# Loading v in one piece a partition, and a new order of steps, in a linear-attention and gated-FFN kernel

## The chip, the cores and the metric

The kernel runs on one core of a Trainium2 chip. A core has five engines with queues of their own: TensorE (PE, matmuls; its weight loads are shown as PEld), VectorE (DVE), ScalarE (ACT), GpSimd (POOL) and SyncE (SP), which here issues all DMAs. The core's 16 DMA engines move data between HBM and the on-chip memory. Each engine works through its instructions in the order in which the program lists them, and waits where an operand isn't ready. The metric is the device time of one execution in microseconds (us), a median of runs; the profile is of one execution.

## What is computed

```python
# q, k, v: (8, 8, 576, 64) float32 (batch, heads, positions, head size)
q_s = exp(q - max(q, axis=-1));  q_s = q_s / (sum(q_s, axis=-1) + 1e-9)
k_s = exp(k - max(k, axis=2));   k_s = k_s / (sum(k_s, axis=2) + 1e-9)
kv  = einsum('bhsd,bhse->bhde', k_s, v)
x   = einsum('bhsd,bhde->bhse', q_s, kv)          # then (B, S, H*D): 4608 tokens x 512
...
xn  = x / sqrt(mean(x * x, axis=-1) + 1e-6) * rms_g
g   = xn @ w_gate                                  # 512 x 1536
out = (g * sigmoid(g) * (xn @ w_val)) @ w_out      # 1536 x 512
```

## The kernel before

The 4608 tokens are nine blocks of 512 (j = 0 to 8), the eight heads four pairs (g = 0 to 3), the eight batches b = 0 to 7 of 576 positions each. A block of tokens needs the key-value products of the one or two batches that it touches, so attention work for later batches and blocks runs between the matmuls of the FFN.

The work is cut into 2,950 named steps (`k_exp.5.1`, `pp.3.0.4` and so on), and a table, `ORDER`, lists them. A step's arguments are numbers, a letter behind a colon names the engine (A for ACT, D for DVE, P for POOL). The kernel records the steps in that order, so `ORDER` alone sets the order on each engine's queue.

**Keys and values.** For a batch b >= 1 and head pair g, `k_load`, `v_load` and `kd_load` bring k, v and a transposed k. Position 5p + i sits in partition p, so a tile has 116 partitions of five positions. `kd` has one buffer, `kt` three, `vt` two. `k_max` (DVE, line 514) takes the maximum of `kd`; `k_rows` spreads it on PE; `k_sub` and `k_exp` (line 539) follow; `k_mm` (PE, line 566) multiplies with v. `k_seg.m` is a `k_mm` and a `k_rows` of neighbouring pairs in one accumulator. The tile of v is (116, 5, 2, 65): the 65th word of each row is a one, so that `k_mm` gives the sum of the keys' exponentials as well. `v_ones` (POOL, line 510) writes the ones, `v_load` (line 507) the 64 words beside them:

```python
nc.sync.dma_start(t[:, :, :, :D], v[b - 1, g].rearrange("p (j h d) -> p j h d", h=2, d=D))
...
nc.gpsimd.memset(v_tile(b, g)[:, :, :, D:], 1.0)
```

In `ORDER` of before, `v_ones` stands ahead of `v_load` of the same tile.

**Queries.** For blocks j >= 2, `q_load` (SP, line 638) brings a 128 x 512 tile (three buffers); `q_max` (DVE, line 697), `q_half`, `q_max2`, `q_sub`, `q_exp` (ACT, line 718), `q_sum`, `q_rec`, `q_mul`, `q_t` (DVE, line 741) make the softmax, `q_hi`, `q_lo`, `q_x` (PE, line 762) the attention output in two halves of precision, `x_sq`, `x_acc` and `n_...` the norm.

**FFN.** Blocks 2 to 8 use products `pp.j.u.n` (PE, line 1132: 12 matmuls, u = 0 to 5 a sixth of the hidden size, n = 1 to 7), evictions `ev.j.u.n` (ACT copies and activations, DVE additions, lines 381, 1147 to 1156), the split of the hidden tile `hu_hi` (ACT), `hu_lo` (DVE or POOL, line 1168), and `fu.j.u.n.k` (PE, line 1180: six matmuls into the output). `ps_gv`, the accumulators of `pp`, are two: a late eviction stops PE two products on. Blocks 0 and 1 use `f1`, `f1p`, `f2` (lines 1195, 1209, 1263); the weights come in the first 95 us (`load_w`, line 422) and are converted, normed and split. `store` (line 1283) brings the output out.

Of the kernel before, what the change touches and what calls it, by code (L numbers as in the profile page):

```python
# [29 lines left out]
k_exp.0.2 k_max.0.3 load_w.0.0 q_eps0.0.0 q_exp.0.1 k_eps.0.2 k_max.0.1 k_exp.0.3 k_mm.0.0 load_w.0.1 q_rec0.0.0  # L30
q_sum0.0.3 q_mul0.0.0:P kv_norm0.0.0:A k_rec.0.2 q_sum0.0.1 k_exp.0.1 q_t0.0.0 load_w.1.1 q_eps0.0.3 k_tr0.2.0
k_eps.0.3 q_c0.0.0:A q_rec0.0.3 k_eps.0.1 k_tr0.2.1 k_rec.0.1 q_mul0.0.3:P k_ev0.2.0 k_rec.0.3 q_x0.0.0 q_max0.0.2
k_ev0.2.1 load_w.1.0 q_eps0.0.1 k_mm.0.2 q_rec0.0.1 q_sub0.0.2:P x_sq.0.0 g_abs k_tr0.3.0 kv_norm0.0.2:A q_mul0.0.1:P
k_tr0.3.1 n_sum0.0 q_exp.0.2 load_w.3.2 k_ev0.3.1 q_sum0.0.2 k_tr0.1.0 conv_mul.0.0 q_eps0.0.2 conv_low.0.0.1
q_rec0.0.2 q_mul0.0.2:P k_ev0.3.0 load_w.2.0 conv_shift.0.0 conv_low.0.1.1 k_tr0.1.1 k_mm.0.3 conv_sign.0.0 k_ev0.1.0
s_tr x_hi.0.0:A s_top load_w.0.2 q_t0.0.3 s_rows q_c0.0.3:A x_lo.0.0 kv_norm0.0.3:A q_t0.0.1 s_bits k_ev0.1.1 k_mm.0.1
load_w.2.1 q_c0.0.1:A q_x0.0.3 conv_low.1.0.2 load_w.1.2 conv_mul.0.1 kv_norm0.0.1:A conv_shift.0.1 x_hi.0.3:A
q_x0.0.1 conv_sign.0.1 kd_load.1.0 x_sq.0.3 q_t0.0.2 x_lo.0.3 w_hi.0.0.2:P conv_mul.1.0 load_w.3.0 q_c0.0.2:A
conv_shift.1.0 x_hi.0.1:A q_x0.0.2 conv_sign.1.0 conv_low.0.2.1 x_lo.0.1 w_lo.0.0:P load_w.4.1 f1.0.0.0.0 conv_mul.1.1
f1.0.0.0.1 f1.0.0.0.3 f1.0.1.0.0 x_hi.0.2:A f1.0.1.0.1 conv_shift.1.1 f1.0.1.0.3 w_lo.0.1:P conv_low.2.0.2 f1.0.0.0.2  # L40
conv_sign.1.1 load_w.2.2 f1.0.0.1.0 f1.0.0.1.1 f1.0.1.0.2 x_lo.0.2 f1.0.1.1.0 w_hi.1.0.2:P conv_mul.0.2 f1.0.1.1.1
n_sq.0.0 conv_shift.0.2 f1.0.0.1.2 f1.0.0.1.3 q_load0.1.0 f1.0.1.1.2 f1.0.0.2.0 conv_sign.0.2 f1.0.0.2.1 x_sq.0.1
f1.0.1.1.3 f1.0.1.2.0 load_w.3.1 k_max.1.0 f1.0.1.2.1 conv_mul.2.0 w_lo.1.0:P n_sum0.1 x_sq.0.2 conv_shift.2.0
f1.0.1.2.2 conv_low.1.2.1 f1.0.1.2.3 w_lo.1.1:P conv_sign.2.0 f1.0.0.2.2 kd_load.1.1 f1.0.0.2.3 conv_low.3.2.1
# [1297 lines left out]
```

## Time and profile before

| what | value |
|---|---|
| median of 3 runs (lowest to highest) | 984.56 us (984.31 to 988.42) |
| the profiled execution, its span | 984.37 us, 982.6 us |
| PE, DVE, ACT, POOL busy | 917.1, 623.3, 573.6, 260.1 us |
| mean granted clock of PE, as a share of full speed | 0.977 |
| DMA packets, of these under 512 B | 57,437, 35,552 |
| moved | 66.18 MB |

The span runs from the first to the last instruction; 1.8 us of the execution lie around it. Busy times are summed instruction by instruction. A bracket behind a row of the timeline tells how long the engine had been idle before it and what ended the wait. An engine's idle time costs only where the end of the program depends on it.

### The profile page before, as it was taken

To read this page: it belongs to the slowest core of one execution; us is meant where nothing else is said; L and a number is where in the kernel's file an instruction comes from. 1 tells how busy PE (TensorE), PEld (TensorE's weight loads), DVE (VectorE), ACT (ScalarE), POOL (GpSimd) and SP (SyncE) were. 2 spreads that over 40 slices of the span, in tenths; PEclk is the share of its full clock that TensorE was granted. 3 is DMA by queue.
4 is the path that set the end of the run, shared out by engine and by line. 5 is a ranking of instruction groups with operands and counts; after the bars stand their busy time and mean duration, and the time that the engine had idled before them with its cause. 6 is when DMAs were issued, how large, how long until landed. Compare 5 with 4: busy or idle time off the path is not lost.

```text
span 982.6 us, 16263 instructions
## 1 busy us (share of the span) xinstructions
PE 917.1 (93%) x6426; PEld 646.1 (66%) x6426; DVE 623.3 (63%) x1350; ACT 573.6 (58%) x896; POOL 260.1 (26%) x263
## 2 busy tenths in 40 slices
PE   8798998999799899778998699999999999999998
PEld 6465876444358677555676477777587776777764
DVE  5786877687588688655665588563868635623322
ACT  6876967896567658554565477463675535433331
POOL 4443764726553222005212020000323101100000
PEclk9897999999999999989999899999999999999999
DMA  9787032112323203222003212010211001000101
GB/s 350 233 256 241 14 89 65 56 47 52 103 72 93 81 21 83 55 70 66 11 12 85 90 36 59 24 44 3 68 25 54 1 1 43 1 1 1 44 1 44
DMA packets 57437, 66.18 MB, mean 67 GB/s; under 512 B 35552, under 2 KB 35808, under 8 KB 57360
## 3 DMA queue, kind: packets, MB, share of 16 engines
q1 hardware_dynamic: 57360, 65.14, 22.2%
q8 instruction: 50, 0.82, 0.3%
q14 instruction: 27, 0.22, 0.1%
HBM read 55.69 MB, written 9.44 MB: 66 GB/s over the span
## 4 chain that ended last, share of the span: by engine, by line
PE 70%; DMA 11%; DVE 10%; ACT 4%; POOL 2%; issue 2%; SPq 1%; DVEq 0%; ACTq 0%; POOLq 0%
PE ps_gv L1132 34%; PE ps_o L1180 19%; DMA qt<-in_q_dram 7%; PE ps_gv L1209 4%; PE ps_gv L1195 4%; PE ps_o L1263 4%; DMA w_o<-in_w_dram 2%; PE ps_a L762 2%; PE ps_a L566 1%; DMA kd<-in_kt_dram 1%; DMA vt<-in_v_dram 1%; DVE sw L703 1%; POOL wf L936 1%; PE ps_gv L456 1%; DVE ps_a L446 1%
## 5 line engine op out<-in xcount | busy, mean ns | idle before, releaser
L1132 PEld LDWEIGHTS <-w_gv 128*128 128x128 f16 x2016 | 197.8, 98 | 43.4 <-issue 6.0
L1132 PE MATMUL ps_gv<-xo,w_gv 128*128 128x256 f16 x1296 | 155.6, 275 | 4.1 <-ACT w_br L381 3.3
L1132 PEld LDWEIGHTS <-w_br 128*128 128x128 f16 x756 | 75.7, 101 | 37.1 <-issue 22.9
L1132 PE MATMUL ps_gv<-x_op,w_gv 128*128 128x256 f16 x720 | 86.6, 273 | 0.0
L1180 PEld LDWEIGHTS <-hh 128*128 128x128 f16 x504 | 49.0, 99 | 51.3 <-issue 4.0
L1132 PE MATMUL ps_gv<-xo,w_br 128*128 128x256 f16 x540 | 69.6, 282 | 13.7 <-DVE wf L1147 6.4
L1180 PEld LDWEIGHTS <-hl 128*128 128x128 f16 x504 | 48.9, 98 | 49.1 <-issue 1.6
L1180 PE MATMUL ps_o<-w_o,hh 128*128 128x512 f16 x336 | 79.5, 380 | 0.0
L1180 PE MATMUL ps_o<-w_o,hl 128*128 128x512 f16 x336 | 79.4, 379 | 0.0
L1195 PE MATMUL ps_gv<-xo,wf 128*128 128x512 f32 x288 | 76.7, 422 | 2.2 <-DVE tm L1224 2.0
L1195 PEld LDWEIGHTS ps_gv<-xo,wf 128*128 128x128 f32 x288 | 56.6, 200 | 18.9 <-issue 4.3
L1132 PEld LDWEIGHTS <-wf 128*128 128x128 f16 x504 | 49.3, 98 | 8.3 <-issue 0.2
L381 ACT COPY ps_gv<-ps_gv 128x512 f32<-128x512 f32 x42 | 24.0, 572 | 49.3 <-PE ps_gv L1132 30.7
L697 DVE TENSOR_REDUCE st<-qt 128x16 f32<-128x512 f32 x28 | 19.0, 680 | 46.8 <-DMA qt<-in_q_dram 46.7
L1132 PE MATMUL ps_gv<-xo,wf 128*128 128x256 f16 x360 | 43.7, 273 | 0.0
L510 POOL MEMSET vt<- 116x10 f32 x28 | 3.2, 117 | 135.6 <-PE ps_a L566 101.5
L1147 DVE TENSOR_TENSOR w_br<-ps_gv,w_br 128x512 f32<-128x512 f32 x29 | 19.9, 688 | 28.5 <-PE ps_gv L1132 24.0
L1132 PE MATMUL ps_gv<-x_op,w_br 128*128 128x256 f16 x216 | 27.8, 280 | 7.7 <-DVE w_br L1147 7.5
L718 ACT ACT_TABLE_LOAD x23 | 29.5, 1283 | 7.7 <-DMA qt<-in_q_dram 7.3
L1209 PE MATMUL ps_gv<-x_op,w_br 128*128 128x512 f16 x144 | 32.4, 379 | 0.0
L1147 DVE TENSOR_TENSOR tm<-ps_gv,tm 128x512 f32<-128x512 f32 x29 | 19.9, 686 | 19.5 <-PE ps_gv L1132 16.4
L566 PE MATMUL ps_a<-vt,kt 115*64 115x65 f32 (+1 forms) x560 | 23.3, 231 | 9.1 <-DMA vt<-in_v_dram 9.1
(336 smaller groups left out, 1945.2 us busy)
## 6 DMA issues: line engine op xcount, KB each, us to landing
w_br<-in_w_dram SPq DMA_DIRECT2D x21, 512.0 KB
qt<-in_q_dram SPq DMA_DIRECT2D x35, 256.0 KB
out_dram<-ot SPq DMA_DIRECT2D x34, 256.0 KB
kt<-in_k_dram SPq DMA_DIRECT2D x28, 290.0 KB
vt<-in_v_dram SPq DMA_DIRECT2D x28, 290.0 KB
kd<-in_kt_dram SPq DMA_DIRECT2D x28, 288.0 KB
w_gv<-in_w_dram SPq DMA_DIRECT2D x10, 512.0 KB
w_o<-in_w_dram SPq DMA_DIRECT2D x5, 512.0 KB
```

The source lines that it names most:

```text
L381: (e.copy if e is nc.scalar else e.tensor_copy)(dst, src)
L446: nc.vector.scalar_tensor_tensor(out=t, in0=t, scalar=3, in1=raw_words(i, a, 1, 0), op0=ALU.logical_shift_left, op1=ALU.bitwise_or)
L566: nc.tensor.matmul(ps[h * D:(h + 1) * D, :n1], lhsT=ke[:n, h, j], rhs=vt_[b, g][:n, j, h], start=(j == 0), stop=(j == len(rows) - 1))
L697: nc.vector.tensor_reduce(out=st, in_=qt_[j, g], axis=AX.X, op=ALU.max)
L718: nc.scalar.activation(qt_[j, g], qt_[j, g], AF.Exp)
L762: nc.tensor.matmul(px[:, c0:c1], lhsT=wt, rhs=mv[:, c0:c1], start=(i == 0), stop=(i == 2))
L1132: nc.tensor.matmul(pair(ps, i), lhsT=a[:, wt], rhs=y if i else y.rearrange("p (a c) -> p a c", a=2), start=(first and k == 0 and i == 0 an ...
L1147: nc.vector.tensor_tensor(out=v, in0=bank[j, u, 5 if n == 5 else 3], in1=v, op=ALU.add)
L1180: nc.tensor.matmul(po[2 * n + t], lhsT=a[:, o:o + P], rhs=w, start=(u == 0 and i == 0 and p == 0), stop=(u == NU - 1 and i == 1 and p == 2))
L1195: nc.tensor.matmul(pd[s], lhsT=m[:, a, c * P:(c + 1) * P], rhs=X[j, c][x], start=(n == 1), stop=(n == 3 * NKT))
L1209: nc.tensor.matmul(pd[s], lhsT=w[:, wt], rhs=x, start=(c == 0 and p == 0), stop=(c == NKT - 1 and p == 2))
L1263: nc.tensor.matmul(po[t], lhsT=a[:, t * P:(t + 1) * P], rhs=w, start=(i == 0 and n == 0), stop=(i == NF - 1 and n == len(terms) - 1))
```

## The change

The host now hands in v with the last word of each row twice, so a row has 65 words and a partition's ten rows are one piece of 650 words, and the load fills the whole tile. The ones are written over the doubled words afterwards, so `v_ones` now stands behind `v_load` in `ORDER` and waits for it. The table `ORDER` is a new one with the same 2,950 steps; some of the small elementwise steps moved between DVE, ACT and POOL (222 named for POOL, before 216).

```diff
 ORDER = """
-exp_table constants kv_zero0.0 warm.9 kd_load.0.0 kv_zero0.1 q_load0.0.3 kv_zero.2 q_load0.0.0 kv_zero.1 kv_zero.3
...
         if b == 0:
             nc.sync.dma_start(v0_(g), v0[g])
         else:
-            nc.sync.dma_start(t[:, :, :, :D], v[b - 1, g].rearrange("p (j h d) -> p j h d", h=2, d=D))
+            nc.sync.dma_start(t.rearrange("p j h d -> p (j h d)"), v[b - 1, g])
...
     rows = np.minimum(5 * np.arange(116)[:, None] + np.arange(5), s - 1)
+    wide = np.minimum(np.arange(d + 1), d - 1)
...
-        "v": pairs(v)[1:, :, :, rows].transpose(0, 1, 3, 4, 2, 5).reshape(b - 1, g, 116, -1),
+        "v": pairs(v)[1:, :, :, rows][..., wide].transpose(0, 1, 3, 4, 2, 5).reshape(b - 1, g, 116, -1),
```

How the new table moves work is shown at three places. In the rows, `kt`, `vt`, `kd` are the tiles of k, v and transposed k, `qt` of q, `out_dram` a store.

The first place is SP's queue while the last sixths of block 2 and the first of block 3 run (390 to 440 us of the trace). Before, from v of (5,1) to q of (5,3):

```order
L507 DMA vt<-in_v_dram 116x10x64
L484 DMA kt<-in_k_dram 116x640
L638 DMA qt<-in_q_dram 128x512
L492 DMA kd<-in_kt_dram 128x576
L484 DMA kt<-in_k_dram 116x640
L507 DMA vt<-in_v_dram 116x10x64
L638 DMA qt<-in_q_dram 128x512
L1283 DMA out_dram<-ot 128x512 x2
L492 DMA kd<-in_kt_dram 128x576
L507 DMA vt<-in_v_dram 116x10x64
L484 DMA kt<-in_k_dram 116x640
L638 DMA qt<-in_q_dram 128x512
```

After, the same engine, from v of (5,1) on:

```order
L508 DMA vt<-in_v_dram 116x650
L485 DMA kt<-in_k_dram 116x640
L639 DMA qt<-in_q_dram 128x512
L508 DMA vt<-in_v_dram 116x650
L485 DMA kt<-in_k_dram 116x640
L493 DMA kd<-in_kt_dram 128x576
L1284 DMA out_dram<-ot 128x512 x2
L639 DMA qt<-in_q_dram 128x512
L508 DMA vt<-in_v_dram 116x650
L485 DMA kt<-in_k_dram 116x640
```

Before, each q load of the stretch stood straight behind a load of v or of v and k; now v and k of (5,2) stand ahead of kd and the stores, and q of (5,2) behind those, while q of (5,1) keeps its place behind v and k.

The second place is SP's queue where block 3 ends and block 4 begins (520 to 560 us of the trace). Before, the loads of k and v for (6,0) to (6,2), then q of (6,2):

```order
L1283 DMA out_dram<-ot 128x512 x2
L484 DMA kt<-in_k_dram 116x640
L507 DMA vt<-in_v_dram 116x10x64
L492 DMA kd<-in_kt_dram 128x576
L507 DMA vt<-in_v_dram 116x10x64
L484 DMA kt<-in_k_dram 116x640
L492 DMA kd<-in_kt_dram 128x576
L484 DMA kt<-in_k_dram 116x640
L507 DMA vt<-in_v_dram 116x10x64
L638 DMA qt<-in_q_dram 128x512
L1283 DMA out_dram<-ot 128x512 x2
```

After, from k of (6,1) to q of (6,2), (6,3) and (7,0):

```order
L508 DMA vt<-in_v_dram 116x650
L485 DMA kt<-in_k_dram 116x640
L639 DMA qt<-in_q_dram 128x512
L493 DMA kd<-in_kt_dram 128x576
L508 DMA vt<-in_v_dram 116x650
L485 DMA kt<-in_k_dram 116x640
L493 DMA kd<-in_kt_dram 128x576
L1284 DMA out_dram<-ot 128x512 x2
L639 DMA qt<-in_q_dram 128x512
L1284 DMA out_dram<-ot 128x512 x2
L639 DMA qt<-in_q_dram 128x512 x2
```

Three loads of v stood in one row ahead of q of (6,2); now that of (6,0) has moved up out of the stretch, and the other two stand apart, each with its k.

The third place is POOL's queue where the last loads of v arrive, at the end of block 5. Before, from the memset for v of (7,2) on:

```order
L510 MEMSET vt 116x10
L849 TENSOR_TENSOR xo<-x_raw,xo 128x512
L829 TENSOR_TENSOR sq<-x_raw 128x512
L510 MEMSET vt 116x10
L849 TENSOR_TENSOR x_op_94<-x_raw,x_op_94 128x512
L833 TENSOR_TENSOR sq<-sq,x_raw 128x512
```

After:

```order
L511 MEMSET vt 116x10
L850 TENSOR_TENSOR x_op_94<-x_raw,x_op_94 128x512
L834 TENSOR_TENSOR sq<-sq,x_raw 128x512
L382 CAST xo<-sq 128x512
L511 MEMSET vt 116x10
L1169 TENSOR_TENSOR hl<-w_br,hl 128x512
L382 CAST x_op_94<-sq 128x512
```

The memset waited for PE's last use of the buffer before and waits for the load now, and the low half of a hidden tile, `hu_lo.5.5.1` (L1169), which PE's `fu.5.5.1.0` reads, now stands right behind the last one.

## Rows read from the trace of the kernel before

**Rows 1.** The page: busy time of each engine; PE's clock in 40 slices, tenths.

```profile
PE 917.1 (93%) x6426; PEld 646.1 (66%) x6426; DVE 623.3 (63%) x1350; ACT 573.6 (58%) x896; POOL 260.1 (26%) x263
PEclk9897999999999999989999899999999999999999
```

**Rows 2.** Stretches: us, busy PE, PEld, DVE, ACT, POOL (count); clock, DMA share, GB/s.

```profile
80.00:100.00 20.00, 15.21 (x50) 10.10 (x49) 14.26 (x25) 14.95 (x21) 5.42 (x5) 0.74 0.58 208
420.00:440.00 20.00, 14.70 (x112) 10.49 (x111) 10.34 (x27) 9.20 (x14) 0.12 (x1) 0.83 0.26 69
600.00:620.00 20.00, 20.00 (x171) 15.30 (x170) 15.09 (x38) 12.42 (x18) 1.17 (x2) 1.00 0.22 59
```

**Rows 3.** Timeline of PE, eight pauses: start, us, instruction, idle before and its releaser.

```profile
241.69 0.80 PE L566 MATMUL ps_a<-vt,kt 116*64 116x65 f32 x20 [1.87 <-DMA vt<-in_v_dram]
251.31 0.80 PE L566 MATMUL ps_a<-vt,kt 116*64 116x65 f32 x20 [2.33 <-DMA vt<-in_v_dram]
342.85 2.71 PE L1132 MATMUL ps_gv<-xo,w_gv 128*128 128x256 f16 x12 [3.28 <-ACT w_br L381]
411.15 2.72 PE L1132 MATMUL ps_gv<-xo,w_br 128*128 128x256 f16 x12 [4.27 <-DVE w_br L1147]
429.75 2.72 PE L1132 MATMUL ps_gv<-xo,w_br 128*128 128x256 f16 x12 [5.30 <-DVE wf L1147]
458.93 2.72 PE L1132 MATMUL ps_gv<-xo,w_br 128*128 128x256 f16 x12 [3.08 <-DVE tm L1147]
533.86 1.33 PE L566 MATMUL ps_a<-vt,kt 116*64 116x65 f32 x20 [4.87 <-DMA vt<-in_v_dram]
556.65 2.72 PE L1132 MATMUL ps_gv<-x_op,w_br 128*128 128x256 f16 x12 [7.47 <-DVE w_br L1147]
```

**Rows 4.** Waits of DVE: us in total, times, longest; one of them in DVE's timeline.

```profile
DVE st L697 <- DMA qt<-in_q_dram: 46.7, 13, 7.3
...
408.42 0.69 DVE L697 TENSOR_REDUCE st<-qt 128x16 f32<-128x512 f32 x1 [5.42 <-DMA qt<-in_q_dram]
```

**Rows 5.** Timeline of SP's DMA issues: start, us that the issue took.

```profile
397.38 0.66 SPq L507 DMA_DIRECT2D vt<-in_v_dram  x1
398.49 3.47 SPq L484 DMA_DIRECT2D kt<-in_k_dram  x1
402.02 0.50 SPq L638 DMA_DIRECT2D qt<-in_q_dram  x1
...
600.68 0.33 SPq L638 DMA_DIRECT2D qt<-in_q_dram  x1
...
698.71 0.66 SPq L507 DMA_DIRECT2D vt<-in_v_dram  x1
699.46 4.17 SPq L484 DMA_DIRECT2D kt<-in_k_dram  x1
```

**Rows 6.** Short stretches in which only k, only v, only q moves.

```profile
243.00:243.50 0.50, 0.50 (x4) 0.25 (x3) 0.43 (x4) 0.00 (x0) 0.11 (x1) 1.00 0.26 102
246.50:247.00 0.50, 0.50 (x4) 0.24 (x3) 0.00 (x0) 0.50 (x2) 0.07 (x1) 1.00 0.34 62
602.00:603.00 1.00, 1.00 (x11) 0.81 (x9) 1.00 (x2) 0.02 (x1) 0.00 (x0) 1.00 0.66 244
```

**Rows 7.** Timeline of PE, twelve matmuls of line 1132 at full clock.

```profile
642.49 1.47 PE L1132 MATMUL ps_gv<-xo,w_gv 128*128 128x256 f16 x12
643.80 1.47 PE L1132 MATMUL ps_gv<-xo,w_br 128*128 128x256 f16 x12
```

**Rows 8.** POOL: its wait at the memset, the memset (min/median/max ns), a split.

```profile
POOL vt L510 <- PE ps_a L566: 101.5, 12, 44.5
...
L510 POOL MEMSET vt<- x28: 108/117/123, 3.4 to 704.7; 116x10 f32 x28
...
521.98 1.49 POOL L1168 TENSOR_TENSOR hh<-wf,hh 128x512 f16<-128x512 f32 x1 [3.28 <-ACT hh L381]
```

**Rows 9.** Timeline of PE, the two longest pauses of the first 100 us.

```profile
41.41 0.60 PE L987 MATMUL ps_a<-kv,ones_b 128*128 128x256 bf16 x4 [2.74 <-DVE y L909]
89.05 1.03 PE L987 MATMUL ps_a<-kv,ones_b 128*128 128x256 bf16 x4 [4.35 <-DVE w_gv L450]
```

More of the change, by code (lines that the diff above doesn't have):

```diff
@@ L30 @@
[L30 to L44, printed above, removed]
@@ new lines @@
+load_w.3.2 q_exp.0.2 k_tr0.1.0 g_abs k_ev0.3.1 k_mm.0.3 q_sum0.0.2 conv_low.0.1.1 k_tr0.1.1 q_eps0.0.2 s_tr
+kv_norm0.0.3:A q_rec0.0.2 load_w.2.0 s_top q_mul0.0.2:P k_ev0.1.0 s_rows q_t0.0.3 s_bits conv_low.0.0.1 q_t0.0.1
+q_c0.0.1:A load_w.0.2 conv_mul.0.0 q_c0.0.3:A conv_shift.0.0 x_hi.0.0:A q_x0.0.3 load_w.2.1 conv_sign.0.0 k_ev0.1.1
+conv_low.1.0.2 x_lo.0.0 k_mm.0.1 conv_mul.0.1 load_w.1.2 kv_norm0.0.1:A conv_shift.0.1 x_hi.0.3:A q_x0.0.1
+conv_sign.0.1 x_sq.0.3 kd_load.1.0 q_t0.0.2 x_lo.0.3 w_hi.0.0.2:P conv_mul.1.0 load_w.4.1 q_c0.0.2:A conv_shift.1.0
@@ new lines @@
+conv_low.8.2.1 conv_shift.6.0 w_hi.5.0.2:P conv_mul.6.1 conv_sign.6.0 n_sq.2.2 kd_load.1.3 conv_shift.6.1 f1.4.0
+load_w.10.1 conv_mul.6.2 conv_sign.6.1 w_lo.5.1:P conv_low.6.2.1 h_mul.3 conv_mul.7.0 conv_shift.6.2 w_lo.5.0:P
+load_w.10.2 n_sq.2.0 f2.3 conv_shift.7.0 conv_sign.7.0 conv_low.8.0.2 conv_sign.6.2 load_w.9.0 conv_mul.7.1
+n_bits.0.1.0 n_bits.0.1.1 conv_mul.7.2 conv_shift.7.1 conv_sign.7.1 f1.4.1 conv_shift.7.2 conv_mul.8.0 load_w.9.1
+conv_sign.7.2 conv_shift.8.0 conv_mul.8.1 load_w.9.2 w_hi.6.0.2:P conv_low.10.0.2 conv_sign.8.0 conv_shift.8.1
@@ new lines @@
+w_lo.9.1:D q_exp.1.1 o_hi.7:A w_lo.8.0:D h_hi.7:A q_sum0.1.1 o_lo.7:P k_mm.1.0 o_hi.8:A q_sum0.1.2 k_rows.1.1
+q_exp.1.3 k_load.1.3 f1.8.0 h_lo.7:P k_eps.1.0 k_rec.1.0 k_sub.1.1 v_load.1.2 kv_norm0.1.0:A q_eps0.1.1 k_exp.1.1
+q_rec0.1.1 o_lo.8:P q_sum0.1.3 k_mm.1.1 q_eps0.1.2 q_rec0.1.2 q_mul0.1.1:P g_mul.8 k_rows.1.2 v_load.1.3 f2.7
+k_eps.1.1 silu.8 q_mul0.1.2:P k_sub.1.2 q_load.2.0 k_load.2.0 k_rec.1.1 kv_norm0.1.1:D v_ones.1.2 w_lo.8.1:P
+q_load.2.1 k_exp.1.2 q_x0.1.0 q_eps0.1.3 o_hi.9:A q_rec0.1.3 t_op.0.0:P k_mm.1.2 x_sq.1.0 q_max.2.0 v_ones.1.3
@@ new lines @@
+t_lo.2.0:D w_sc.4.0 o2_lo.4 f2.13 b_hi.4.0:A q_max.2.3 b_hi.4.1:P o2_hi.8 h_mul1.15 w_sc.3.1 b_lo.4.0:P k_max.3.1
+b_hi.3.2:A q_x.2.0 kd_load.3.2 o2_lo.2 h_hi.15:A f2.14 b_lo.3.2:D o2_hi.6 h_lo.15:D o2_hi.3 o2_lo.6 b_hi.3.3:A
+x_raw.2.0 o2_lo.3 f2.15 o2_hi.5 b_lo.3.3:D o2_hi.7 o_bits.8 o2_lo.5 w_sc.4.1 kv_lo.1.3 kv_lo.1.2 f1p.16.1 o2_lo.8
+w_sc.3.0 kv_lo.1.1 b_lo.4.1:D b_hi.3.0:A o2_lo.7 b_hi.3.1:A w_sc.5.0 b_lo.3.0:D f1p.17.0 h_mul1.16 b_lo.3.1:P
+b_hi.5.0:A x_sq.2.0 b_lo.5.0:D h_hi.16:A f1p.17.1 t_op.4.0:D silu1.17 h_lo.16:D w_sc.5.1 t_op.2.1:D b_hi.5.2:A
@@ new lines @@
+k_eps.4.2 k_rec.4.2 ev.3.0.8 q_max.5.0 kv_hi.4.2:A k_sub.4.3 pp.3.0.5 hu_lo.2.5.0:P x_raw.4.0 k_max.5.2 pp.3.0.6
+x_sum.3.4:P kv_lo.4.2 kd_load.5.3 k_exp.4.3 q_x.4.1 q_sub.4.2:D v_ones.5.0 ev.3.0.2 k_seg.12 hu_lo.2.5.1:D
+o_x_hi.3.6:A q_exp.4.2 k_eps.4.3 o_x_lo.3.6:P pp.3.0.7 k_rec.4.3 v_load.5.1 k_sub.5.0 kv_hi.4.3:A k_load.5.2 q_sum.4.2
+x_raw.4.1 fu.2.4.0.0 ev.3.0.3 q_half2.4.2 k_exp.5.0 ev.3.0.5 pp.3.0.4 x_sq.4.1 q_sum2.4.2 v_ones.5.1 q_rec.4.2
+q_mul.4.2:D pp.3.0.3 q_t.4.2 x_acc.4.1:P q_half.4.3 ev.3.0.9 q_load.5.1 k_seg.13 q_hi.4.2:A ev.3.0.6 pp.3.1.1
@@ new lines @@
+pp.6.1.1 ev.6.0.11 ev.6.0.6 hu_hi.6.0.1 q_x.7.1 ev.6.0.10 ev.6.1.0 k_seg.24 q_hi.7.2:A hu_lo.6.0.1:D pp.6.1.2
+hu_hi.6.0.0 q_lo.7.2:D x_raw.7.1 hu_lo.6.0.0:D pp.6.1.6 x_sq.7.1 k_eps.7.3 k_rec.7.3 q_t.7.3 ev.6.1.8 x_acc.7.1:P
+q_max.8.1 q_x.7.2 kv_hi.7.3:A q_load.8.2 ev.6.1.2 kv_lo.7.3 pp.6.1.5 q_half.8.1 x_sq.7.2 q_hi.7.3:A q_max2.8.1
+x_acc.7.2:D pp.6.1.7 x_raw.7.2 q_lo.7.3:D q_sub.8.1:D q_x.7.3 ev.6.1.3 q_t.8.0 pp.6.1.4 x_sq.7.3 ev.6.1.5 q_load.8.3
+x_raw.7.3 x_acc.7.3:P q_max.8.2 pp.6.1.3 ev.6.1.9 ev.6.1.11 n_hi.7:A pp.6.2.1 n_lo.7:D hu_hi.6.1.1 ev.6.1.6
@@ new lines @@
+hu_lo.6.5.1:D fu.6.2.0.1 fu.6.3.0.0 hu_hi.6.4.0 hu_lo.6.4.0:D fu.6.3.0.1 ev.7.0.2 pp.7.0.7 hu_hi.6.5.0 hu_lo.6.5.0:D
+fu.6.4.0.0 ev.7.0.3 ev.7.0.5 pp.7.0.4 pp.7.0.3 ev.7.0.9 ev.7.0.11 pp.7.1.1 ev.7.0.6 ev.7.0.10 q_x.8.1 ev.7.1.0
+fu.6.4.1.1 q_hi.8.2:A x_sq.8.1 q_lo.8.2:D pp.7.1.2 x_raw.8.1 x_acc.8.1:D hu_hi.7.0.1 q_t.8.3 q_x.8.2 ev.7.1.8
+hu_lo.7.0.1:P pp.7.1.6 x_sq.8.2 q_hi.8.3:A x_acc.8.2:D pp.7.1.5 x_raw.8.2 q_lo.8.3:D ev.7.1.2 q_x.8.3 pp.7.1.7
+x_sq.8.3 x_raw.8.3 x_acc.8.3:D fu.6.4.0.1 ev.7.1.3 n_hi.8:A ev.7.1.5 fu.6.5.0.0 hu_hi.7.0.0 n_lo.8:P pp.7.1.3
@@ new lines @@
+hu_lo.7.0.0:D n_sum.8 ev.7.1.6 fu.6.5.0.1 ev.7.1.10 n_t.8 store.6.0 pp.7.2.1 store.6.1 hu_hi.7.1.0 n_y0.8
+hu_lo.7.1.0:P pp.7.1.4 n_y1.8 fu.6.5.1.0 ev.7.1.9 ev.7.2.0 n_rows.8 fu.6.5.1.1 x_nrm.8.0:D x_nrm.8.1:D store.6.2
+pp.7.2.6 store.6.3 x_nrm.8.3:P o_x_hi.8.0:A pp.7.2.2 ev.7.2.2 o_x_lo.8.0:D x_nrm.8.2:D pp.7.2.7 ev.7.2.8 x_sum.8.1:D
+o_x_hi.8.1:A ev.7.1.11 pp.7.2.5 ev.7.2.3 o_x_lo.8.1:D o_x_hi.8.3:A pp.7.2.4 hu_hi.7.1.1 x_sum.8.3:D o_x_lo.8.3:D
+o_x_hi.8.4:A fu.7.0.0.0 ev.7.2.5 hu_lo.7.1.1:P ev.7.2.9 pp.7.3.1 o_x_lo.8.4:D x_sum.8.2:D pp.7.2.3 ev.7.2.11
@@ L296 @@
+ev.8.5.10 fu.8.2.0.1 hu_lo.8.5.1:D fu.8.3.0.0 hu_hi.8.4.0 hu_lo.8.4.0:D fu.8.3.0.1 fu.8.4.1.0 hu_hi.8.5.0
+hu_lo.8.5.0:D fu.8.4.1.1 fu.8.5.1.0 fu.8.5.1.1 store.8.2 fu.8.4.0.0 store.8.3 fu.8.4.0.1 fu.8.5.0.0 fu.8.5.0.1
+store.8.0 store.8.1
 """
```

484 lines of the change are left out of this document (229 added, 255 removed).

## The prediction, made before the changed kernel ran

> **What bounds the kernel now.** I read first the busy line and the clock line of the page [rows 1]. TensorE (PE) is busy 917.1 of 982.6 us, so 65.5 us are idle on it, and the clock line has six slices under full. Everything else has room: VectorE (DVE) 63%, ScalarE (ACT) 58%, GpSimd (POOL) 26%. Then the table by stretch [rows 2]: 600 to 620 us is full (20.00 of 20 busy, clock 1.00), while 420 to 440 us has 14.70 busy at a mean clock of 0.83, and 80 to 100 us looks alike (15.21, 0.74). So the kernel is bound by PE where PE has work, and what can be won is pauses and half-clock time, in the first 100 us and from 240 to 560 us. From 560 us on there is next to nothing to win.
>
> Then PE's own timeline, for the idle time in brackets [rows 3]. Eight pauses carry the middle: 1.87, 2.33, 3.28, 4.27, 5.30, 3.08, 4.87 and 7.47 us, together 32.5 us, half of all idle time. Three of them name the load of v at once. The others name ACT or DVE evictions, and DVE's rows tell why those were late [rows 4]: DVE runs in order, stands 5.42 us at the first reduction of a q tile (line 697) until its load lands at 408.42, and the eviction that PE needs is queued behind it. That wait occurs 13 times and sums to 46.7 us.
>
> Why the q loads are late is on SP's queue [rows 5]. A load of v takes 0.66 us to issue, and the load behind it is held: the issue of k took 3.47 us, where one with nothing of v ahead takes 0.33 us (600.68), so q could start only at 402.02 and landed 6.4 us later (408.42). It is so behind most loads of v, late ones too (699.46: 4.17 us). The transfers are slow as well [rows 6]: while only v moves, 62 GB/s; while only k moves, 102 GB/s; a q load moves at 244 GB/s. The k and v transfers follow one another and don't overlap (k's rate in the row at 243 us, v's in the one at 246.5 us), and q's last pieces come behind them.
>
> After a long pause PE also runs slowly: the first 12 matmuls after five of the pauses take 2.71 or 2.72 us where the same 12 take 1.47 us at full clock [rows 3, 7], that is the 1.2 GHz level in place of 2.4. After the pauses of 1.87 and 2.33 us the 20 small matmuls took 0.80 us, after the one of 4.87 us 1.33 us: short pauses here did not cost the clock, pauses from 3.08 us on did.
>
> **The change, part by part.** *Load of v as one piece a partition.* Before, a load is 116 x 10 pieces of 256 B, 297 KB; now 116 pieces of 2600 B, 302 KB. k's load (116 pieces of 2560 B) is the nearest row in every respect, so I take its rate: 302 KB at 102 GB/s is 2.96 us, against 297 KB at 62 GB/s, 4.8 us. Bounds: no better than now (4.9 us), or as fast as q (1.2 us). The issue behind it falls from about 4 us to the 0.33 us of the free queue [rows 5].
>
> DMA shares weigh on how far to trust that. v's rows show 0.34 of 16 engines, 5.4 engines' worth, k's 0.26, or 4.2 [rows 6]; read so, v might keep a few more engines than k. The Trainium skill (DMA: Bandwidth & Descriptors, section on why a DMA increments its semaphore by 16) says that a load uses the largest number of engines up to 16 that divides its outer size, which for 116 rows is 4, and the lowest-numbered ones. By that, one piece a partition gains no engine, and k and v go on queueing for the same four. The trace agrees for k (4.2 engines' worth) and in that the two don't overlap. By 5.4 engines a load would take 2.3 us instead of 2.96, some 3 us over the whole kernel.
>
> A burst of v, k and q, as at 397 us, then goes: three issues 1.0 us, 0.9 us until packets move (an estimate: q issued at 600.68 is in full flow in the row from 602 us [rows 5, 6]), v 2.96, k 2.9, the rest of q about 1.0: q lands 8.8 us after v's issue. Now it is 408.42 - 397.38 = 11.0 us. So with the old order each burst gains 2 to 3 us, more where two v loads stand close.
>
> *New order.* Here the table matters more. The first and second place of the order (section on the change) show SP: q loads stand further from v, and v loads further from one another. I counted the PE groups (12 matmuls, 1.31 us from start to start in rows 7; a group of six at the output is as long) between a step's load of v and the q reduction that waits. For the pause at 342.85 (v 4.2, q 4.1) they were about 5, now 9; at 411 (v 5.1, q 5.1) 3, now 7 and an attention segment (about 10 us, over the 8.8 needed); at 429.75 (v 5.2, q 5.2) the two stood together, now about 15 us apart; for 533.86 and 556.65 three loads of v (6.0 to 6.2) stood within 6 us of PE work with q 6.2 behind them, now they are 35 and 28 us apart, and q 6.2's reduction comes 9 us after v 6.2. What stays tight: q 6.1 (2 us behind v 6.1, reduction after 6.5 us of work: 8.8 - 6.5 = 2.3 us short) and q 5.3 (reduction 2.6 us after its issue, k and v 6.0 just ahead: about 1.5 us short). I leave 1.5 us for places I can't see. So of 32.5 us, 5.3 stay and 27 go. Bounds: the new order is no better than the old (about 8 stay by the 2 to 3 us a burst, more if v gains less, up to 20) and all go.
>
> *Clock.* Five groups of 12 lose 1.24 us each, 6.2 us at least [rows 3, 7]. The row 420:440 loses up to 0.17 x 14.7 = 2.5 us for its long pause alone [rows 2], so 6 to 12 us, and I take 9. With pauses under 3 us most comes back: 7 us.
>
> *The ones.* The memset of the two ones a row is 0.117 us, 28 times, on POOL [rows 8]. Before, it stood ahead of the load and POOL waited there 101.5 us in all for PE's last use of the buffer. Now it stands behind the load and waits until v has landed, in most places 2.6 us of PE work after the issue, so POOL stands 1 to 4 us each time. POOL is 74% idle and what it loses is the old wait of 101.5 us; what is queued behind is mostly needed 5 us of PE work later or more. One place is tight: at the third place of the order the low half of the hidden tile (5,5,1), about 1.49 us on POOL [rows 8], stands right behind the last memset, and PE's use is one group (1.31 us) later. Cost 0 to 3 us there; I take it as in the 1.5 us above. The load itself no longer waits for a memset but for PE directly, which gains nothing much.
>
> *Engines.* Six more small steps on POOL in all, at up to 1.49 us each [rows 8]: off the path while it is 74% idle. *First 180 us.* Two v loads stand among the weight loads (DMA full there) and each held the queue 3 to 4 us. The pauses at 41 and 89 us (2.74, 4.35 us [rows 9]) wait for converted weights or the norm. The order there is moved only a little. Freed queues speak for a gain of some us, and v (1,2), whose matmuls now come 4.8 us of PE work after its issue instead of 18, for a loss of up to 3; I take 0, bounds -6 to +6.
>
> Sum: 984.4 (the profiled execution; median of the runs 984.56) - 27 - 7 = 950 us.
>
> **Rivals.** *Half the gain* (967 us, 958 to 978). q still queues behind k and v; the new order spends the time that the loads gain, by packing loads nearer elsewhere, or DVE (15.09 of 20 us busy even at 600 us [rows 2]) takes over as the late engine. For it: the reductions stand 1.5 to 4.1 us of PE work after the q issue in 18 of 28 cases, and an unhindered load needs about 2.4 us (600.68 to 603 [rows 5, 6]). Against: the loads of v are spread. Half of 34 is 17. By the skill's rule on engine counts (same page) the shared four engines are its mechanism.
>
> *More gain* (938 us, 930 to 942). The new order also closes the early pauses and the clock loss behind them, 12 us more. For it: a clock of 0.74 there [rows 2]; against: the weight loads limit that part.
>
> *Slower, by the memset* (995 us, 980 to 1005). POOL now stands still until a load lands. If PE needed POOL's next result soon after in most places, each of 28 loads would cost PE about 1.6 us: 28 x 1.6 = 45 us, more than the gain of 34: 950 + 45 = 995 us. It decides from 1.2 us a load on. For it: POOL is in order, and the one tight place. Against: the order shows one such place only.
>
> *It doesn't do what it says* (982 us, 976 to 988): the 2600 B rows are still cut small, v stays at 62 GB/s, and only the order acts. k's row of 2560 B speaks against it.
>
> **How the numbers follow.** Forecast 950 (942 to 958): 0.50. Half the gain: 0.25. More gain: 0.12. No effect: 0.05. Slower: 0.08. The forecast's bounds are those of the pauses and the clock. To hold 8 in 10: the low end at 935 keeps most of the larger gain, the high end at 975 most of the half gain; left out are slower, no effect and the tails. Faster by over 0.5% (under 979.6; about what a measurement of this kernel can tell from no change): 0.50 + 0.12 + 0.24 and a little of "no effect", 0.87. Within: 0.05. Slower by over 0.5%: 0.08.
>
> **What would show it.** Right: about 28,000 packets instead of 57,437, none of v's under 512 B; issues behind v of 0.3 us; v moving at about 100 GB/s; DVE's wait at q's first reduction well under 46.7 us; PE idle 37 to 40 us instead of 65.5, no or one pause over 3 us after 240 us, and a mean clock of 0.985 or more. Wrong: PE pauses that name POOL, or the memset's wait for v in front of a late hidden tile (the slower rival); the same DVE wait with q landing 8 us after v (half the gain); pauses at new places, for DVE or ACT, with the loads early (the order is worse than I read it).

## The result, and the profile after

The changed kernel takes 959.55 us (median of 4 runs, 957.89 to 965.07) where the kernel before takes 985.98 (984.31 to 988.42, 4 runs): a ratio of 0.974, with a 95% interval of 0.969 to 0.979. The prediction was 950 us in a range of 935 to 975; of a gain of 34 us, 26 came. By the forecasts one by one, 959.55 lies 1.6 us above the bounds of the main one (942 to 958) and inside those of the rival *half the gain* (958 to 978). The profiled execution is the slowest of the four (965.07 us, span 963.3), which matters below.

The page of the changed kernel, busy line, clock line and DMA packets, which answer to [rows 1]:

```profile
PE 919.5 (95%) x6426; PEld 646.2 (67%) x6426; DVE 623.8 (65%) x1346; ACT 571.1 (59%) x892; POOL 265.6 (28%) x269
PEclk9789899899989999999999999999999999999999
DMA packets 28206, 66.31 MB, mean 69 GB/s; under 512 B 3073, under 2 KB 3329, under 8 KB 28129
```

PE is idle for 963.3 - 919.5 = 43.8 us instead of 65.5, packets are halved, and from the thirteenth slice of the clock line on (289 us) no digit is under 9. What is left stands early. The same stretches of both kernels (us, busy time of PE, PEld, DVE, ACT, POOL; clock, DMA share, GB/s), before and then after:

```profile
60.00:130.00 70.00, 64.78 (x298) 47.98 (x297) 51.13 (x91) 53.39 (x79) 40.80 (x39) 0.93 0.53 165
130.00:200.00 70.00, 63.67 (x351) 42.27 (x350) 52.62 (x119) 54.61 (x85) 39.62 (x38) 1.00 0.24 66
310.00:600.00 290.00, 260.40 (x2030) 192.15 (x2028) 198.52 (x471) 169.13 (x259) 59.67 (x59) 0.95 0.20 55
```

```profile
60.00:130.00 70.00, 64.29 (x287) 46.18 (x285) 54.80 (x94) 52.65 (x79) 40.20 (x38) 0.95 0.51 161
130.00:200.00 70.00, 61.60 (x309) 41.62 (x309) 45.62 (x100) 50.78 (x78) 37.51 (x35) 0.95 0.22 71
310.00:600.00 290.00, 282.98 (x2322) 212.67 (x2321) 223.91 (x524) 188.89 (x289) 66.08 (x67) 1.00 0.20 63
```

From 310 to 600 us PE was idle for 29.6 us at a clock of 0.95; now 7.0 us, at 1.00. From 60 to 200 us it is no better than before. The PE pauses of after that are worth a look, against [rows 3] and [rows 9]:

```profile
94.86 0.61 PE L988 MATMUL ps_a<-kv,ones_b 128*128 128x256 bf16 x4 [3.89 <-DVE w_gv L451]
...
268.59 0.50 PE L763 MATMUL ps_a<-qh,kv 128*128 128x256 f32 x2 [2.42 <-ACT qh L382]
270.83 0.58 PE L763 MATMUL ps_a<-ql,kv 128*128 128x256 f32 x1 [1.74 <-POOL vt L511]
...
493.83 1.47 PE L1133 MATMUL ps_gv<-xo,wf 128*128 128x256 f16 x12 [2.15 <-DVE tm L1148]
```

Behind 100 us no pause is over 2.5 us, where seven were over 3 (six of [rows 3] and one of 3.36 us at 167.24 us), and the longest pause of the middle, 2.15 us, is followed by 12 matmuls at full speed (1.47 us).

Two milestones show that time was lost ahead of the middle: the first product of block 1 (`f1p`) and the first of block 2 (`pp`), before and then after, from PE's timeline:

```profile
173.89 3.70 PE L1209 MATMUL ps_gv<-x_op,w_bx 128*128 128x512 f16 x16 [0.43 <-ACT x_op L381]
...
284.07 1.47 PE L1132 MATMUL ps_gv<-xo,w_bx 128*128 128x256 f16 x12
```

```profile
183.03 3.57 PE L1210 MATMUL ps_gv<-x_op,w_bx 128*128 128x512 f16 x8 [0.53 <-ACT x_op L382]
...
297.55 1.47 PE L1133 MATMUL ps_gv<-xo,w_bx 128*128 128x256 f16 x12
```

At the first of block 2 the changed kernel is 13.5 us behind; it gains 32.8 from there (982.6 - 284.1 = 698.5 us of span against 963.3 - 297.6 = 665.7) and ends 19.3 ahead in these two executions.

SP's issues, a short stretch in which a load of v moves, with one of k queued behind it, and the two waits, against [rows 4 to 6] and [rows 8]:

```profile
249.88 0.26 SPq L508 DMA_DIRECT2D vt<-in_v_dram  x1
250.19 0.34 SPq L485 DMA_DIRECT2D kt<-in_k_dram  x1
...
248.50:249.00 0.50, 0.36 (x7) 0.19 (x8) 0.47 (x2) 0.50 (x2) 0.28 (x1) 1.00 0.26 104
...
POOL vt L511 <- DMA vt<-in_v_dram: 130.5, 20, 31.6
DVE st L698 <- DMA qt<-in_q_dram: 33.2, 10, 7.2
```

The issue behind v takes 0.34 us, v moves at 104 GB/s, and POOL waits 130.5 us for v where it waited 101.5 us for PE. All of that is as forecast. DVE's wait for q was to be well under 46.7 us and is 33.2 us, ten times.

### The profile page after: what moved, and what is told of

Read it like the earlier page. It is cut to its first block, busy times and chain, and to the rows that moved or that the text cites. A ratio compares the mean times of both kernels' runs of the same rounds, so it can differ in the third digit from the quotient of the medians.

```text
span 963.3 us, 16295 instructions
## 1 busy us (share of the span) xinstructions
PE 919.5 (95%) x6426; PEld 646.2 (67%) x6426; DVE 623.8 (65%) x1346; ACT 571.1 (59%) x892; POOL 265.6 (28%) x269
## 4 chain that ended last, share of the span: by engine, by line
PE 72%; DVE 10%; DMA 10%; ACT 4%; issue 2%; POOL 1%; SPq 0%; ACTq 0%; POOLq 0%; DVEq 0%
PE ps_gv L1133 33%; PE ps_o L1181 18%; DMA qt<-in_q_dram 5%; PE ps_gv L1210 5%; PE ps_gv L1196 5%; PE ps_o L1264 4%; PE ps_a L763 2%; DMA w_br<-in_w_dram 2%; DMA vt<-in_v_dram 2%; PE ps_a L567 1%; DMA w_o<-in_w_dram 1%; PE ps_gv L457 1%; DVE x_raw L794 1%; PE ps_o L692 1%; PE ps_a L527 1%
## 5 line engine op out<-in xcount | busy, mean ns | idle before, releaser
L1133 PE MATMUL ps_gv<-xo,w_br 128*128 128x256 f16 x540 | 65.7, 273 | 0.0
L382 ACT COPY ps_gv<-ps_gv 128x512 f32<-128x512 f32 x42 | 24.0, 572 | 47.4 <-PE ps_gv L1133 33.7
L698 DVE TENSOR_REDUCE st<-qt 128x16 f32<-128x512 f32 x28 | 18.9, 675 | 33.3 <-DMA qt<-in_q_dram 33.2
L511 POOL MEMSET vt<- 116x10 f32 x28 | 3.1, 117 | 133.9 <-DMA vt<-in_v_dram 130.5
L1169 POOL TENSOR_TENSOR hl<-wf,hl 128x512 f16<-128x512 f32 x5 | 5.8, 1157 | 104.0 <-ACT hl L382 104.0
L1148 DVE TENSOR_TENSOR w_br<-ps_gv,w_br 128x512 f32<-128x512 f32 x29 | 19.9, 688 | 21.4 <-PE ps_gv L1133 19.5
L719 ACT ACTIVATE qt<-qt 128x512 f32<-128x512 f32 x35 | 22.0, 628 | 15.5 <-POOL qt L715 6.9
L1133 PEld LDWEIGHTS <-w_bx 128*128 128x128 f16 x252 | 24.6, 98 | 4.2 <-issue 0.4
```

What stands on the lines that cost most here:

```text
L382: (e.copy if e is nc.scalar else e.tensor_copy)(dst, src)
L698: nc.vector.tensor_reduce(out=st, in_=qt_[j, g], axis=AX.X, op=ALU.max)
L719: nc.scalar.activation(qt_[j, g], qt_[j, g], AF.Exp)
L1133: nc.tensor.matmul(pair(ps, i), lhsT=a[:, wt], rhs=y if i else y.rearrange("p (a c) -> p a c", a=2), start=(first and k == 0 and i == 0 an ...
L1148: nc.vector.tensor_tensor(out=v, in0=bank[j, u, 5 if n == 5 else 3], in1=v, op=ALU.add)
```

## Experiments

All times are medians; ratios are against runs of the kernel before on the same chip, whose medians are 985.8 to 987.0 us. "Idle" is PE's idle time from 310 to 600 us, a fixed stretch of time that holds not quite the same work in each; the milestone is the first product of block 2, each from the profiled execution. One execution's milestone is good to some 4 us only: e3 and e5, and e6 and e10, list the same steps and loads up to it and lie 4.3 and 3.4 us apart.

| kernel | order | load of v | us | ratio (95%) | first `pp` | idle |
|---|---|---|---|---|---|---|
| before | old | 1160 pieces | 985.8 to 987.0 | | 284.1 | 29.6 |
| changed | new | 116 pieces | 959.55 | 0.974 (0.969 to 0.979) | 297.6 | 7.0 |
| e1 | new | 1160 | 986.4 | 1.0005 (0.999 to 1.002) | 306.6 | 15.8 |
| e2 | old | 116, no ones | 954.59 | 0.969 (0.965 to 0.973) | 277.1 | 14.9 |
| e3 | old | 116 | 957.48 | 0.970 (0.967 to 0.973) | 281.3 | 15.8 |
| e4 | old, then new from block 1 | 116 | 952.05 | 0.966 (0.963 to 0.969) | 282.9 | 7.2 |
| e5 | old, then new from block 2 | 116 | 946.69 | 0.959 (0.957 to 0.962) | 277.0 | 7.4 |
| e6 | old | 116, cut 112 + 4 rows | 929.58 | 0.942 (0.940 to 0.945) | 270.3 | 1.1 |
| e7 | old | 580 | 974.13 | 0.987 (0.984 to 0.991) | 284.1 | 21.4 |
| e8 | old | 1160, ScalarE's queue | 970.11 | 0.984 (0.979 to 0.988) | 288.4 | 17.6 |
| e9 | new | 116, cut 112 + 4 | 932.15 | 0.945 (0.941 to 0.949) | 269.1 | 2.3 |
| e10 | old, then new from block 2 | 116, cut 112 + 4 | 931.44 | 0.944 (0.940 to 0.948) | 266.9 | 2.3 |
| e11 | old | 1160, cut 112 + 4 | 930.40 | 0.942 (0.939 to 0.945) | 269.0 | 2.5 |
| e12 | new | 116, no ones | 960.08 | 0.973 (0.970 to 0.977) | 294.9 | 6.3 |

### Which half of the change carries the gain

e1 is the new table with the old load:

```diff
-            nc.sync.dma_start(t.rearrange("p j h d -> p (j h d)"), v[b - 1, g])
+            nc.sync.dma_start(t[:, :, :, :D], v[b - 1, g].rearrange("p (j h d) -> p j h d", h=2, d=D))
```

> The new order with the load of v as before (116 x 10 pieces of 256 B). Theory 1 (the load's form carries the gain after 300 us, some 30 us, and the new order costs about 9 us ahead of that): the next issue behind v is held 4 us again, the pauses over 3 us come back, 975 to 995 us. Rival (the spacing of loads in the new order carries it): 958 to 968 us, few pauses over 3 us after 240 us.

e2 and e3 are the old table with the new load. In e2 the steps `v_ones` are left out, in e3 each stands halfway between its load and the matmuls that use it:

```diff
-v_ones.4.2 v_load.4.2 ... k_seg.11
+v_load.4.2 ... v_ones.4.2 ... k_seg.11
```

> The old order with v in one piece a partition; the memsets of the ones are left out (so the sums of the keys are not formed). Theory 1: the start as before (first output product of block 2 at about 308 us), the rest 25 to 32 us shorter, 950 to 960 us, faster than the changed kernel or equal. Rival (spacing carries it): 967 to 975 us, with pauses of 2 to 4 us where q stands behind v and k.

> As e2 but with the memsets, each halfway in the table between the load of v and its matmuls. Theory 1: the memset costs nothing where it stands late, 950 to 962 us, within 4 us of e2. Rival (the memset behind the load holds GpSimd and through it TensorE): 10 us or more over e2.

The load alone gives 985.79 to 957.48 us (e3), 28 us, as much as the whole change; the new table alone gives nothing (e1: 986.4). But the table does move time. The stretch of the middle and the first product of block 2, in e1 and then in e3 (columns as above, and PE's timeline), show where:

```profile
310.00:600.00 290.00, 274.20 (x2221) 204.10 (x2218) 219.26 (x508) 183.04 (x283) 67.97 (x67) 0.99 0.22 62
...
306.61 1.47 PE L1133 MATMUL ps_gv<-xo,w_bx 128*128 128x256 f16 x12
```

```profile
310.00:600.00 290.00, 274.22 (x2221) 205.83 (x2220) 212.09 (x500) 180.55 (x275) 58.16 (x58) 0.99 0.19 58
...
281.32 1.47 PE L1133 MATMUL ps_gv<-xo,w_bx 128*128 128x256 f16 x12
```

With the old load the new table brought the middle from 29.6 us of idle time to 15.8, and lost 22 us ahead of it (306.6 against 284.1). With the new load it brought the middle from 15.8 (e3) to 7.0 us and lost 16 (297.6 against 281.3). Both halves act on the middle alike: each alone leaves 15.8 us. The times of all three fell in the ranges of theory 1, but two of its details failed. The loss ahead of block 2 was larger than the 9 us that it named, and e2's start was not as before: its first output product of block 2 (`fu`) came at 300.6 us, in the kernel before at 308.0. In e1 only two pauses over 3 us came back behind 240 us (7.37 and 4.14 us), where the kernel before has six.

### Where the new order loses

e4 and e5 take the steps of the old table (that of e3) up to a point and the rest in the order of the new one. Their tables are written out; in outline, but for the places of a few `v_ones`, they are

```python
order = old[:cut] + [s for s in new if s not in old[:cut]]     # cut at f1p.12.0.0 (e4), at pp.2.0.1 (e5)
```

> The old order up to the first product of block 1 (173.9 us in the trace of before, 183.0 in that of the changed kernel), the new order behind it, v in one piece. Theory 1: the start's loss of 9 us is the order's and comes back, 946 to 954 us. Rival (the loss is a half-clock stretch that comes and goes from run to run, or is spent again later): 956 to 962 us.

> The old order up to the first product of block 2, the new one behind it, v in one piece, memsets late in the old part. If the new order loses some 8 us between the first product of block 1 and the first of block 2 (the traces: 114.5 us in the changed kernel, 113.7 with the old start, 106.4 in the old order with the new load) and gains 9 us behind it: 943 to 949 us, faster than all so far. Rival (what is gained behind rests on attention work that the new order did earlier): 950 to 957 us.

Both fell in the range of the first expectation: 952.05 and 946.69 us. So with loads as in the changed kernel the new order was worse ahead of block 2 and better behind it: by the medians, e5 is 12.9 us under the changed kernel, from which it differs ahead of block 2, and 10.8 us under e3, from which it differs behind. A few us of the changed kernel's start are chance: in its profiled execution 20 to 40 us ran at a clock of 0.66, in e1 and e9 at 1.00, though none of the three issues a load in which it differs from the others before 35 us; the first matmuls on the weights began at 33.7 us there, at 29.7 and 29.9 in e1 and e9. This is the row of after and then the one of e9:

```profile
20.00:40.00 20.00, 16.51 (x80) 10.32 (x81) 12.88 (x26) 16.08 (x29) 8.15 (x7) 0.66 0.56 215
```

```profile
20.00:40.00 20.00, 15.63 (x84) 9.37 (x81) 14.98 (x28) 19.28 (x35) 8.22 (x7) 1.00 0.72 260
```

### What a load of v costs

e7 cuts the load into five pieces a partition, leaving out each fifth's last word, which the memset writes; e8 issues the old load from ScalarE's queue:

```diff
-            nc.sync.dma_start(t.rearrange("p j h d -> p (j h d)"), v[b - 1, g])
+            nc.sync.dma_start(t.rearrange("p j h d -> p j (h d)")[:, :, :2 * D + 1],
+                              v[b - 1, g].rearrange("p (j d) -> p j d", j=CH)[:, :, :2 * D + 1])
...
-            nc.sync.dma_start(t[:, :, :, :D], ...)
+            nc.scalar.dma_start(t[:, :, :, :D], ...)
```

> As the old order with the new load and late memsets (957.5 us), but v in five pieces of 516 B a partition, 580 a load in place of 116 or 1160. Theory hold (the time that the issue behind v is held goes by the number of pieces): held about 2 us, 966 to 974 us. Rival (only pieces under some size cost, by the rate): v at about 100 GB/s, next issue at 0.3 us, 955 to 961 us.

> The kernel before (v in 256 B pieces, old order) with the loads of v issued from ScalarE's queue, so that SP's is not held by them. If the held queue is most of the cost: 960 to 970 us, next issue on SP after v at 0.3 us, q landing 4 us earlier. Rival (the slow transfer on shared engines is most of it): 976 to 988 us, q as late as before. ScalarE itself may wait at the issue, which would show as its idle time in front of the load.

e7's SP queue, v and then the held issue of k:

```profile
326.17 0.66 SPq L508 DMA_DIRECT2D vt<-in_v_dram  x1
326.88 2.01 SPq L485 DMA_DIRECT2D kt<-in_k_dram  x1
```

The hold goes by the number of pieces: about 4 us at 1160, 2.0 to 2.3 at 580, 0.34 at 116; the time, 974.13 us, lies between those of before and e3, 0.1 us above the hold theory's range. The rate goes with the size as well, 59 to 62, 73 and 104 GB/s (73 in e7 while only v moves, at 698 us), so e7 alone doesn't part them.

In e8 SP is free (0.28 us for k, 0.33 for q behind a load of v), and some 17 of e3's 28 us come: 970.11 us, 0.1 us outside the first expectation; DVE's wait for q falls from 46.7 to 22.1 us. What the loads of v did to SP they now do to ScalarE. This is ScalarE's queue and then PE's timeline of e8, with the longest pause of the kernel:

```profile
514.23 6.77 ACTq L507 DMA_DIRECT2D vt<-in_v_dram  x1
521.10 0.63 ACT L386 ACTIVATE kv<-ps_a,rs 64x64 fp32r<-64x64 f32 x2 [7.28 <-issue]
...
526.26 1.03 PE L566 MATMUL ps_a<-vt,kt 116*64 116x65 f32 x14 [9.56 <-DMA vt<-in_v_dram]
```

So the hold was a real cost, but not all of it; how much of the rest is the slow transfer and how much the hold's new place on ScalarE, e8 does not part.

### Four DMA engines or sixteen

e6 keeps the old order and the one-piece load, with late memsets, and cuts each load of v and of k by rows:

```diff
-            nc.sync.dma_start(t.rearrange("p j h d -> p (j h d)"), v[b - 1, g])
+            u = t.rearrange("p j h d -> p (j h d)")
+            nc.sync.dma_start(u[:112], v[b - 1, g, :112])
+            nc.sync.dma_start(u[112:], v[b - 1, g, 112:])
...
-        nc.sync.dma_start(t, k[b - 1, g])
+        nc.sync.dma_start(t[:112], k[b - 1, g, :112])
+        nc.sync.dma_start(t[112:], k[b - 1, g, 112:])
```

> The old order with v in one piece and memsets late (957.5 us), and each load of v and of k cut in two by rows, 112 and 4. Theory: 116 rows are carried by four DMA engines, 112 by sixteen; the transfers of v and k fall from 3 us to about 1 and the q load behind them lands 3 to 4 us earlier: k and v move at over 200 GB/s, idle time between 310 and 600 us falls from 15.8 to under 9 us, 944 to 952 us. Rival (the transfers no longer matter, or the two more issues a pair eat the gain): 954 to 961 us.

It took 929.58 us, 28 us under e3 and far under the range expected: the first product of block 2 came 11.0 us earlier as well (270.3 against 281.3), which the expectation had not counted. A stretch in which only v moves, and the middle of the kernel:

```profile
651.00:651.50 0.50, 0.50 (x7) 0.45 (x5) 0.49 (x3) 0.23 (x1) 0.24 (x1) 1.00 1.06 234
...
310.00:600.00 290.00, 288.92 (x2342) 216.86 (x2340) 221.51 (x522) 189.57 (x287) 56.82 (x58) 1.00 0.20 58
```

All 16 engines are busy (share 1.06), v moves at 234 GB/s, and PE is idle for 1.1 us of 290. Then the other half of the question: is the number of pieces of any account with 16 engines? e11 is the kernel before, 256 B pieces and early memsets, with the same cut:

> The kernel before, v still in 256 B pieces and memsets ahead of the loads, only the loads of v and k cut into 112 and 4 rows. If the number of DMA engines is most of what a load costs: v's 1120 pieces over 16 engines take 1.5 us or less, the hold behind them shrinks with them, 930 to 942 us. Rival (the pieces themselves hold the queue, whatever the engines): next issue behind v still 3 to 4 us, 955 to 972 us.

It took 930.40 us. Its SP queue behind a load of v, and a stretch in which only v moves:

```profile
287.13 0.61 SPq L509 DMA_DIRECT2D vt<-in_v_dram  x1
287.79 0.67 SPq L510 DMA_DIRECT2D vt<-in_v_dram  x1
288.51 0.50 SPq L484 DMA_DIRECT2D kt<-in_k_dram  x1
...
652.00:652.50 0.50, 0.50 (x4) 0.24 (x3) 0.47 (x4) 0.50 (x2) 0.50 (x1) 1.00 1.02 231
```

With 70 pieces an engine instead of 290 the issue behind the two parts of v takes 0.50 us here, 0.36 to 0.91 elsewhere, and 256 B pieces move at 231 GB/s. So neither the size nor the number of the pieces was the cause by itself: they cost where four engines carry them all. One piece a partition is one way to lower the cost, 16 engines is the other, and with the second the first gives nothing (929.58 against 930.40). What the cut of k and that of v are worth apart was not tried: e6 and e11 cut both.

The Trainium skill has the rule for the count of engines (DMA: Bandwidth & Descriptors, section on why a DMA increments its semaphore by 16; the rules for kernel authors there say to put a size that is a multiple of 16 outermost). By it 116 rows go over 4 engines and 112 rows over 16; the traces agree: shares of 0.26 (the changed kernel) and 1.06 (e6).

e9 and e10 apply the cut to the changed kernel and to e5:

> The changed kernel with each load of v and k cut into 112 and 4 rows. If what the new order loses ahead of block 2 is the order's own, the first product of block 1 stays at 178 to 184 us (169.2 in the old order with the same loads) and the time is 933 to 942 us, above the old order's 929.6. Rival (the new order's start only suffered from late loads): 922 to 929 us.

> The old order up to the first product of block 2 and the new one behind it, loads cut into 112 and 4. The old order with such loads has 1.1 us idle between 310 and 600 us, so little is left for the new order to gain: 926 to 931 us, equal to the old order's 929.6. Rival (the new order's part still gains some of its 9 us): 919 to 925 us.

932.15 and 931.44 us, the first 0.9 us under its first range and above the rival's, the second 0.4 us above its first range: with wide loads no order is better than the old one by more than the intervals, and none much worse. Ahead of block 2 the new table now costs 0.7 us (e9 against e10), where with four-engine loads it cost 12.9 (the changed kernel against e5). The milestone says the same of e9: its first product of block 1 came at 166.1 us (169.2 in e6), where the expectation had 178 to 184 if the loss were the order's own. Its first product of block 2, from PE's timeline:

```profile
269.08 1.47 PE L1136 MATMUL ps_gv<-xo,w_bx 128*128 128x256 f16 x12
```

That is 28.5 us ahead of the changed kernel with the same table, some 4 us of it the clock at 20 to 40 us, and near e6 (270.3, clock 0.83 at 20 to 40 us) and e10 (266.9, clock 1.00). So the new table's loss at the start came from how it places loads that take four engines, and 2.2 us of it at most from the order of work as such. e6 and e11 are the fastest kernels of the study, 5.8% under the kernel before and 3% under the changed one.

### The price of the memset

e12 is the changed kernel without the steps `v_ones`:

> The changed kernel without the memsets of the ones (so the sums of the keys are not formed). In the changed kernel's trace three pauses of TensorE name the memset, 4.2 us together; if that is its price: 954 to 957 us. Rival (GpSimd's 130 us of waiting at the memset delays other steps too and costs 8 us or more): 945 to 951 us. Other rival (nothing): 958 to 961 us.

960.08 us against 959.55: nothing, although POOL's 130.5 us of waiting at the memset are gone. The three pauses that name the memset were filled by the next late thing (at 266.9 us in e12 PE waits 3.49 us for ScalarE). In the old order e2 and e3 differ by 2.9 us, within their intervals.

## Why the prediction came out as it did, point by point

**What bounds the kernel: right, with two readings off.** Pauses of PE behind late q loads, and the slow clock behind long pauses. Where loads came early (e6), idle time in the middle went from 29.6 to 1.1 us and the clock stayed at 1.00. The clock line of before has four slices under 9, not six. And the length of a pause alone does not tell whether the clock falls, as the reading "pauses from 3.08 us on did" has it: the kernel before kept 1.00 through one of 3.36 us,

```profile
167.24 0.60 PE L987 MATMUL ps_a<-kv,ones_b 128*128 128x256 bf16 x4 [3.36 <-DVE y L909]
...
160.00:180.00 20.00, 14.82 (x79) 9.93 (x78) 17.73 (x35) 17.95 (x28) 12.37 (x12) 1.00 0.21 55
```

while in e7 the 12 matmuls behind pauses of 2.36 and 2.52 us took 2.71 and 2.72 us, and those behind one of 2.80 us 1.47 us.

**The load in one piece: right in its prices, not in what it leaves.** 302 KB at k's rate was taken (102 GB/s); measured 104. The issue behind it was put at 0.33 us; measured 0.34. With the old order each pause was to lose 2 to 3 us, and in e3 six of the eight lost 1.8 to 2.8 us, one 1.5 us and one nothing. But of 32.5 us about 8 were to stay, and 18.4 stayed. The sum was short by its own terms: 2 to 3 us off each of the eight leave 10 to 17 us. e3's 28 us hold more than those pauses: the clock in the middle rose from 0.95 to 0.99, and the first product of block 2 came 2.8 us earlier.

**The engine count: weighed and left.** The rule of the Trainium skill by which 116 rows take four engines was held against a reading of 5.4 from v's share; the rule was right, and the prediction used it for 3 us, as a limit on the gain, and as the mechanism of one rival. That it also names the cause of the late q loads, and that 112 rows would take it away, was not seen; e11, which changes nothing else, puts some 56 us on it (986.1 to 930.4).

**New order in the middle: right in the sum, by luck in the split.** It was to bring the eight pauses from about 8 us left to 5.3. Measured, as idle time of the middle: 15.8 us in e3, 7.0 in the changed kernel. So the load took less than forecast and the table more, and the two errors nearly cancel. "Here the table matters more" was not borne out: in the middle each half alone takes 13.8 us off the 29.6, and over the whole kernel the table alone gives nothing (e1). The places that were counted as cleared are cleared, and the tightest stayed as forecast: DVE waits 3.69 us for q 6.1, and PE then stands 2.15 us (493.83 us, above), where 2.3 us was forecast.

```profile
490.24 0.69 DVE L698 TENSOR_REDUCE st<-qt 128x16 f32<-128x512 f32 x1 [3.69 <-DMA qt<-in_q_dram]
```

At q 5.3, which was to be 1.5 us short, DVE waits 4.18 us (to 456.91 us) and PE does not stand at all.

**First 180 us: the term that was mis-sized.** I took 0 with bounds of -6 to +6, from two arguments, a freed queue and one pair of v that is used early. The measured term, up to the first product of block 2, is +13.5 us in the profiled execution, +16 against the old order with the same loads (e3), +12.9 by the medians (against e5); some 4 us of the first, and a part of the second, are the clock of that one execution. Of the 13.5 us, 9.1 had come by the first product of block 1 and 4.3 came behind it: the loss reached to 300 us, where I had ended it at 180. I had counted q's distances behind 240 us step by step and had not counted the loads at the start, where the new table issues two loads of v back to back among the weight loads, and k, v and q within 6 us at 126 us. That loads on four engines are the cause is shown by e9, in which the loss is gone; which of them costs which pause was not told apart.

**Clock: right for the middle, not in the sum.** 7 of 9 us were to come back, and from 310 to 600 us all of it did (0.95 to 1.00). But the start lost as much: 20 to 40 us went from 1.00 to 0.66, 130 to 200 us from 1.00 to 0.95. PE's busy time over the profiled execution rose from 917.1 to 919.5 us. So of the sum's 27 us of pauses and 7 of clock, 21.7 and -2.4 came there; the other three executions are 4.6 to 7.2 us shorter, at clocks of 0.984 to 0.988.

**The memset: right.** POOL waits longer than before (130.5 us) and it costs nothing that e12 can tell. Three pauses of PE do name it (1.39, 1.06 and 1.74 us), which was to be a sign of the slower rival; without it other late work fills them. At the tight place, behind the last memset, PE has no pause at all.

**Rivals.** *It doesn't do what it says* and *slower, by the memset* fell by the packets and e12. *More gain* needed the early pauses to close; they opened. *Half the gain* (967 us, 958 to 978, which holds the result) had the right mechanism, q still queueing behind k and v on the same four engines: DVE's wait for q fell by less than a third, to 33.2 us. It stood in the changed kernel beside the cleared pauses, and the result lies between its 967 us and the forecast's 950.

**The signs.** Named right: packets, issues, v's rate, no pause over 3 us after 240 us. Not met: idle time 43.8 instead of 37 to 40 us, a clock of 0.979 in the profiled execution instead of 0.985 (0.984 to 0.988 in the other three).
